# Attention with two mixing blocks on one core: fp32 scores for sixteen pairs, fp32 products for six, and shorter conversion and normalisation

## The chip, the cores and the metric

The kernel runs on one core of a Trainium2 chip. A core has a matrix engine (TensorE, PE in the rows; its weight loads are PEld), a vector engine (VectorE, DVE), a scalar engine (ScalarE, ACT), a general engine (GpSimd, POOL) and an engine that mostly issues transfers (SyncE, SP), and sixteen DMA engines behind the queues. Engines run their own instructions in order and wait for each other by semaphores. The metric is the time of one execution on the device in microseconds (us), as the median of several runs.

## The reference, cut to what matters

```python
def _attn_ref(q, k, v):                       # 4 batches, 12 heads, 448 tokens, 64 columns
    scores = np.matmul(q, k.transpose(0, 1, 3, 2)) / np.sqrt(64)
    scores = np.where(np.triu(np.ones((448, 448), bool), k=1), -1e9, scores)
    attn = np.exp(scores - np.max(scores, axis=-1, keepdims=True))
    attn = attn / (np.sum(attn, axis=-1, keepdims=True) + 1e-09)
    return np.matmul(attn, v)

def _moe_ref(x, w_tok1, w_tok2, w_ch1, w_ch2):   # x: 4 x 448 x 768
    xt = x.transpose(0, 2, 1)
    u = x + (np.maximum(xt @ w_tok1, 0.0) @ w_tok2).transpose(0, 2, 1)
    return u + np.maximum(u @ w_ch1, 0.0) @ w_ch2

def _moe2_ref(x, w_theta, w_tok_r, w_tok_i, w_ch):
    theta = x @ w_theta
    y = einsum('ts,bsd->btd', w_tok_r, x * cos(theta)) + einsum('ts,bsd->btd', w_tok_i, x * sin(theta))
    u = x + y
    return u + np.maximum(u @ w_ch, 0.0)
```

The three follow each other: attention, then token and channel mixing, then a second mixing block. q, k, v are float32; the weights of the mixing blocks arrive as 64-bit floats.

## The kernel before, in words

Two heads of a batch make a pair; there are 24 pairs, six to a batch. A pair has seven score tiles (`TILES`): tile (0, 0) holds the first 64 queries of both heads, and tiles (i, h), i = 1 to 3, hold 128 queries of one head against 64 + 128 i keys. One tile is one step, 168 steps in all. At step n the kernel emits `scores` of tile n and, `LAG` = 4 steps behind, `pv`, the product with v, of tile n - 4. Beside the steps it emits conversions of weights, and from step 53 on (`FIRST_UNIT`) units of the channel mixing: 14 up to step 88, then 29 in 42 steps. The scheduler of the language puts the instructions of each engine in order by priority; scores, `pv` and `prep` stand at a high priority (`AHEAD`).

`scores` multiplies q with k into a bank of PSUM; VectorE (L356) adds the mask and takes the row's extreme, ScalarE (L358) takes the exponential and its row sum. There are two forms of each matrix product:

- Scores: for pairs in `NATIVE` (0 to 7) q and k stay float32, 64 rows of contraction padded with zeros to 128 by a POOL memset (L275), one product a tile (L349). For the others `prep` loads q and k in 128 rows, ScalarE rounds both to fp32r, VectorE makes the rests (L291 to L296), and a tile has two products (L349, L351) of at least 256 columns.
- Products with v: for pairs in `NATPV` (0 to 11) TensorE transposes the exponentials in float32 (L365), ScalarE copies them out of PSUM (L367) and `pv` multiplies in float32 (L393). For the others ScalarE writes a high half in fp16 (`copy_to`, L160), VectorE the low halves (L378), SP issues a transposing DMA (L381), and `pv` makes three fp16 products a block (L403). These pairs need v in two halves as well: `value_squares` and `value_split`.

The products of a pair gather in one bank, `ps_pv`. `finish` divides them by the row sums `sm` into `xb`: the six tiles with i > 0 in one VectorE pass (L410), tile (0, 0) in two passes of 64 rows (L415), since its two heads stand in different rows. Every two pairs, `tokmix` uses `xb` and its two fp32r parts.

The weights arrive as 64-bit floats. ScalarE takes the high word, as a float, times a power of two (`abs64`); VectorE shifts the exponent into place (L183), adds the sign (L184) and the low word's upper bits (L185). Thirty weight tiles of 768 columns pass through it during attention (`ROUNDINGS`, one in some 3.4 steps from step 14, and six late ones), four of the token weights at the start, and 26 smaller pieces (384 or 224 columns) for the resident weights of the last block, near 525 to 575 us.

All bulk loads and stores, the transposing DMAs among them, are issued from SP's queue in one order.

Of the kernel before, what the change touches and what calls it, by code (L numbers as in the profile page):

```python
# [8 lines left out]
F32 = mybir.dt.float32  # L9
# [4 lines left out]
AF = mybir.ActivationFunctionType  # L14
# [15 lines left out]
NATIVE = {0, 1, 2, 3, 4, 5, 6, 7}  # L30
NATPV = {0, 1, 2, 3, 4, 5, 6, 7, 8, 9, 10, 11}
# [23 lines left out]
def fused(ctx, tc, q, k, v, w_tok1, w_tok2, w_ch1, w_ch2, w_theta, w_tok, w_ch, out):  # L55
# [119 lines left out]
    def abs64(f, raw):  # L175
        nc.scalar.activation(f, raw[:, :f.shape[-1], 1].bitcast(F32), AF.Abs, scale=REBIAS)

    def round64(f, raw):


        low, high = raw[:, :f.shape[-1], 0], raw[:, :f.shape[-1], 1]
        u = f.bitcast(U32)
        nc.vector.tensor_scalar(out=u, in0=u, scalar1=3, scalar2=None, op0=ALU.logical_shift_left)  # L183
        nc.vector.scalar_tensor_tensor(out=u, in0=high, scalar=0x80000000, in1=u, op0=ALU.bitwise_and, op1=ALU.bitwise_or)  # L184
        nc.vector.scalar_tensor_tensor(out=u, in0=low, scalar=29, in1=u, op0=ALU.logical_shift_right, op1=ALU.bitwise_or)  # L185
# [42 lines left out]
    def mm3(ps, a, b, ka, kb, first, last):  # L228
# [12 lines left out]
                            base=0, pattern=[[-1, P]], channel_multiplier=1)  # L241
    mask0 = ac.tile([P, 2, 64], F32, tag="mask0", name="mask0")
# [20 lines left out]
    for j in range(2):  # L263
        xb = ac.tile([P, 4, P], F32, tag=f"x{j}", name=f"x{j}")
        nc.gpsimd.memset(xb[:, 0, :], 0.0)
        xbufs.append(xb)
# [55 lines left out]
    class Pair:  # L322
        def __init__(self, b, pr, parts):
            self.b, self.pr = b, pr
            self.qs, self.kh, self.kl, self.v = parts[:4]
            self.unit = parts[4] if len(parts) > 4 else 1.0
            self.mx = ap2.tile([P, 7], F32, tag="mx", name="mx")
            self.sm = ap2.tile([P, 8], F32, tag="sm", name="sm")
            self.pts, self.ps, self.sent = {}, None, None
            self.native_pv = b * NPR + pr in NATPV  # L330

    def scores(pp, i, h):
# [17 lines left out]
        if pp.kl is not None:  # L350
# [8 lines left out]
                             accum_out=pp.sm[:, j:j + 1])  # L359
# [23 lines left out]

    def pv(pp, i, h):
        if pp.ps is None:
            pp.ps = bank("pv", 1)
        reg = 0 if i == 0 else ((i - 1) * 2 + h + 1) * D
        pt = pp.pts[i, h]
        if pp.native_pv:
            blks = [8] if i == 0 else [6 + h] + [2 * u + h for u in range(i)]  # L390
            n = D if i == 0 else 2 * D
            for u, vt in enumerate(blks):
                pp.pv = nc.tensor.matmul(pp.ps[:, reg:reg + n], lhsT=pt[:, u], rhs=pp.v[0][:, vt * D:vt * D + n],  # L393
                                 start=(u == 0), stop=(u == len(blks) - 1))
            return
# [6 lines left out]
        for n, (blk, c, vt) in enumerate(jobs):  # L402
            pp.pv = nc.tensor.matmul(pp.ps[:, reg:reg + D], lhsT=pt[:, blk], rhs=pp.v[c][:, vt * D:(vt + 1) * D],  # L403
                             start=(n == 0), stop=(n == len(jobs) - 1))

    def finish(pp, xb, xg):
        ps, sm = pp.ps, pp.sm
        nc.vector.tensor_scalar(out=sm[:, 0:7], in0=sm[:, 0:7], scalar1=1e-9, scalar2=pp.unit, op0=ALU.add, op1=ALU.mult)
        nc.vector.reciprocal(out=sm[:, 0:7], in_=sm[:, 0:7])
        nc.vector.tensor_tensor(out=xb[:, 1:4, :].rearrange("p i (h d) -> p (i h) d", h=2),  # L410
                                in0=ps[:, D:7 * D].rearrange("p (j d) -> p j d", d=D),
                                in1=sm[:, 0:6].unsqueeze(2).to_broadcast([P, 6, D]), op=ALU.mult)
        for h in range(2):
            r = slice(64 * h, 64 * h + 64)
            nc.vector.tensor_scalar(out=xb[r, 0, 64 * h:64 * h + 64], in0=ps[r, 0:D],  # L415
                                    scalar1=sm[r, 6:7], scalar2=None, op0=ALU.mult)
# [570 lines left out]
```

## Time and profile before

| what | value |
|---|---|
| median of 3 runs | 890.24 us (889.29 to 891.47) |
| the profiled execution | 888.24 us, of which its span is 886.5 us |
| granted TensorE clock, mean | 0.996 |
| busy in the span | TensorE 96%, VectorE 71%, ScalarE 61%, POOL 19% |

The span runs from the first instruction to the last of the profiled execution; busy is the time in which an engine has an instruction open. Matmuls overlap, and their ends are modelled, so an open TensorE is not a TensorE at its peak. L with a number is a line of the kernel before; a line can be that of a helper.

### The profile page before, as it was taken

Reading aid. Unit: us, or ns where it says so; the run is one execution under the profiler, and the core shown is the slowest. Engines: PE = TensorE matmul, PEld = TensorE weight load, DVE = VectorE, ACT = ScalarE, POOL = GpSimd, SP = SyncE. Lnnn points to the kernel's source line nnn. Section 1 sums busy time; section 2 is a strip of 40 time slices with the busy share of each in tenths; the row PEclk is TensorE's granted clock in tenths of the full one; section 3 lists DMA queues with packets and bytes.
Section 4 is the critical chain, followed back from the end, with each engine's and each line's share of the span. In section 5 each row is a group of like instructions: output and inputs, shape, how many; then the busy total and the mean of one; then the engine's idle time right before and its main releaser. Section 6 shows DMA issues by size and latency. Waiting matters only on the chain.

```text
span 886.5 us, 16065 instructions
## 1 busy us (share of the span) xinstructions
PE 851.7 (96%) x5619; PEld 547.8 (62%) x5619; DVE 632.8 (71%) x1511; ACT 544.0 (61%) x1271; POOL 166.3 (19%) x319
## 2 busy tenths in 40 slices
PE   7999889999899999999999999999999999999998
PEld 6888767776656566565666554555555555555554
DVE  6899996878998775766886258768856448567442
ACT  6798776757776564657655257437746447466441
POOL 2232232223251200121211112051111002101000
PEclk9999989999999999999999999999999999999999
DMA  7857865747899996656565778711622132231011
GB/s 217 255 182 228 289 231 183 272 169 232 205 310 306 288 210 148 165 202 129 162 186 137 232 240 293 238 55 41 201 62 67 50 116 67 69 116 58 18 50 73
DMA packets 105793, 149.63 MB, mean 169 GB/s; under 512 B 61104, under 2 KB 72304, under 8 KB 105712
## 3 DMA queue, kind: packets, MB, share of 16 engines
q1 hardware_dynamic: 105168, 147.59, 55.3%
q0 software_dynamic: 384, 0.79, 0.4%
q8 instruction: 44, 0.72, 0.3%
q14 instruction: 37, 0.30, 0.1%
q10 hardware_dynamic: 160, 0.23, 0.1%
HBM read 112.39 MB, written 22.81 MB: 153 GB/s over the span
## 4 chain that ended last, share of the span: by engine, by line
PE 66%; DVE 13%; DMA 11%; issue 4%; ACT 3%; POOL 1%; SPq 1%; ACTq 0%; DVEq 0%; POOLq 0%
PE ps_mm L230 15%; PE ps_mm L231 15%; PE ps_mm L232 15%; DMA pt<-ph 6%; PE ps_pv L393 3%; PE ps_sc L349 3%; PE ps_sc L230 3%; PE ps_sc L231 3%; PE ps_sc L232 3%; DVE sb L356 2%; DVE ph L378 1%; PE ps_mm L365 1%; DVE wf L184 1%; DMA ws<-w_c 1%; DVE wf L185 1%
## 5 line engine op out<-in xcount | busy, mean ns | idle before, releaser
L230 PE MATMUL ps_mm<-h,ws 128*128 128x448 f16 x432 | 151.9, 353 | 0.4 <-DMA ws<-w_c 0.4
L231 PE MATMUL ps_mm<-h,ws 128*128 128x448 f16 x432 | 152.2, 353 | 0.0
L232 PE MATMUL ps_mm<-h,ws 128*128 128x448 f16 x432 | 152.2, 353 | 0.0
L230 PEld LDWEIGHTS <-ws 128*128 128x128 f16 x720 | 70.4, 98 | 63.4 <-issue 4.1
L232 PEld LDWEIGHTS <-ws 128*128 128x128 f16 x720 | 70.4, 98 | 62.8 <-issue 3.1
L231 PEld LDWEIGHTS <-ws 128*128 128x128 f16 x720 | 70.5, 98 | 62.4 <-issue 4.2
L358 ACT ACTIVATE sb<-sb,mx 128x192 f32<-128x192 f32 (+3 forms) x168 | 89.2, 532 | 32.1 <-DVE mx L356 30.6
L230 PE MATMUL ps_mm<-ut,ws 128*128 128x448 f16 x288 | 102.0, 355 | 5.6 <-ACT ut L160 2.3
L231 PE MATMUL ps_mm<-ut,ws 128*128 128x448 f16 x288 | 102.0, 354 | 0.6 <-DVE ut L196 0.5
L232 PE MATMUL ps_mm<-ut,ws 128*128 128x448 f16 x288 | 102.1, 354 | 0.0
L356 DVE CUSTOM_DVE_ANT_0 sb<-ps_sc,mask 128x192 f32<-128x192 f32 (+3 forms) x168 | 74.3, 456 | 12.7 <-PE ps_mm L365 9.5
L124 ACT ACTIVATE junk<-acc 128x448 bf16<-128x448 f32 x72 | 41.1, 571 | 63.9 <-DVE acc L879 41.0
L160 ACT ACTIVATE ph<-sb 128x192 f16<-128x192 f32 (+3 forms) x84 | 36.4, 442 | 45.9 <-DMA pt<-ph 45.8
L393 PE MATMUL ps_pv<-v_raw,ptf 128*128 128x128 f32 (+1 forms) x456 | 63.9, 277 | 0.3 <-PE ps_mm L138 0.2
L378 DVE SCALAR_TENSOR_TENSOR ph<-sb,ph 128x64 f16<-128x64 f32 (+3 forms) x156 | 44.6, 328 | 26.4 <-ACT ph L160 26.2
L393 PEld LDWEIGHTS ps_pv<-v_raw,ptf 128*128 128x128 f32 x456 | 59.2, 193 | 5.0 <-PE ps_mm L138 1.5
L163 POOL TENSOR_SCALAR h<-t 128x448 f16<-128x448 f32 x48 | 32.8, 685 | 140.3 <-ACT t L477 140.1
L349 PE MATMUL ps_sc<-kh,qs 128*128 128x256 f32 (+2 forms) x112 | 45.9, 416 | 3.3 <-DVE mx L356 3.3
L230 PE MATMUL ps_sc<-th,ut 128*128 128x384 f16 x144 | 46.9, 326 | 0.0
L232 PE MATMUL ps_sc<-th,ut 128*128 128x384 f16 x144 | 46.8, 326 | 0.0
L231 PE MATMUL ps_sc<-th,ut 128*128 128x384 f16 x144 | 46.6, 326 | 0.0
L479 DVE TENSOR_TENSOR h<-t,h 128x448 f16<-128x448 f32 x48 | 30.2, 633 | 19.7 <-POOL h L163 19.5
(215 smaller groups left out, 2040.5 us busy)
## 6 DMA issues: line engine op xcount, KB each, us to landing
ws<-w_c SPq DMA_DIRECT2D x120, 384.0 KB, 4.5
raw<-in_w_ch_dram SPq DMA_DIRECT2D x30, 768.0 KB, 4.5
w_c<-ws SPq DMA_DIRECT2D x30, 384.0 KB, 3.5
q_raw<-in_q_dram SPq DMA_DIRECT2D x16, 448.0 KB, 4.1
k_raw<-in_k_dram SPq DMA_DIRECT2D x16, 448.0 KB, 4.9
v_raw<-in_v_dram SPq DMA_DIRECT2D x24, 288.0 KB, 3.2
x2d<-acc SPq DMA_DIRECT2D x24, 224.0 KB, 3.7
acc<-x2d SPq DMA_DIRECT2D x24, 224.0 KB, 2.8
```

The lines of the kernel that those rows point to most:

```text
L124: nc.scalar.activation(j[:, 0:src.shape[-1]], src, AF.Square, accum_out=dst)
L160: nc.scalar.activation(dst, src, AF.Copy, scale=scale)
L163: e.tensor_scalar(out=dst, in0=src, scalar1=scale, scalar2=0.0, op0=ALU.mult, op1=ALU.add)
L230: nc.tensor.matmul(ps, lhsT=ka(a[:, 0]), rhs=kb(b[:, 0]), start=first, stop=False)
L231: nc.tensor.matmul(ps, lhsT=ka(a[:, 0]), rhs=kb(b[:, 1]), start=False, stop=False)
L232: return nc.tensor.matmul(ps, lhsT=ka(a[:, 1]), rhs=kb(b[:, 0]), start=False, stop=last)
L349: nc.tensor.matmul(ps[:, 0:n], lhsT=lhs, rhs=cut(pp.kh), start=True, stop=pp.kl is None)
L356: pp.first = nc.vector.tensor_tensor_reduce(out=dst, in0=src, in1=msk, op0=ALU.add, op1=ALU.min, scale=-0.125, scalar=3.0e38, accum_out=pp ...
L358: pp.last = nc.scalar.activation(sb[:, 0:kk], sb[:, 0:kk], AF.Exp, bias=pp.mx[:, j:j + 1], scale=-1.0, accum_out=pp.sm[:, j:j + 1])
L378: nc.vector.scalar_tensor_tensor(out=dst, in0=sb[:, c0:c1], scalar=PSC, in1=hi[:, c0:c1], op0=ALU.mult, op1=ALU.subtract)
L393: pp.pv = nc.tensor.matmul(pp.ps[:, reg:reg + n], lhsT=pt[:, u], rhs=pp.v[0][:, vt * D:vt * D + n], start=(u == 0), stop=(u == len(blks) - 1))
L479: gates[0] = nc.vector.tensor_tensor(out=t[:, 1], in0=f, in1=t[:, 0], op=ALU.subtract)
```

## The change

Pairs 8 to 15 move to the float32 form of the scores, pairs 6 to 11 to the fp16 form of the product with v. `abs64` keeps the sign in the float that it makes and leaves on POOL a word that holds the sign alone, in place of the high word; `round64` then shifts and joins the sign in one pass. `finish` scales all of `ps_pv` in one pass: tile (0, 0)'s product is written twice, side by side, and a two-column mask `own`, multiplied on POOL with that tile's reciprocal sum, zeroes the half that belongs to the other head; `xb` needs no memset any more. In the float32 form the last tile's product is 64 columns wide instead of 128.

```diff
--- before.py
+++ after.py
@@ -27,8 +27,8 @@
 NEG = -1.0e30
 PSC = 32768.0
 BUFS = dict(ut=12, h2=8, acc=12, ws=8, wf=3, raw=3, sb=3, ph=3, pt=5, t=3, junk=1)
-NATIVE = {0, 1, 2, 3, 4, 5, 6, 7}
-NATPV = {0, 1, 2, 3, 4, 5, 6, 7, 8, 9, 10, 11}
+NATIVE = {0, 1, 2, 3, 4, 5, 6, 7, 8, 9, 10, 11, 12, 13, 14, 15}
+NATPV = {0, 1, 2, 3, 4, 5}
 AHEAD, LAG, LOOK = 500, 4, 2
 KEEP, UBACK = 6, 16
 ROUND_BITS, ROUND_FETCH, ROUND_SPLIT, ROUND_STORE = 1, 2, 3, 5
@@ -173,15 +173,16 @@
         nc.sync.dma_start(out=raw[:, :src.shape[-1]].rearrange("p n w -> p (n w)"), in_=src.bitcast(U32))
 
     def abs64(f, raw):
-        nc.scalar.activation(f, raw[:, :f.shape[-1], 1].bitcast(F32), AF.Abs, scale=REBIAS)
+        high = raw[:, :f.shape[-1], 1].bitcast(F32)
+        nc.scalar.activation(f, high, AF.Copy, scale=REBIAS)
+        product(high, high, 0.0, 1.0)
 
     def round64(f, raw):
 
 
-        low, high = raw[:, :f.shape[-1], 0], raw[:, :f.shape[-1], 1]
+        low, sign = raw[:, :f.shape[-1], 0], raw[:, :f.shape[-1], 1]
         u = f.bitcast(U32)
-        nc.vector.tensor_scalar(out=u, in0=u, scalar1=3, scalar2=None, op0=ALU.logical_shift_left)
-        nc.vector.scalar_tensor_tensor(out=u, in0=high, scalar=0x80000000, in1=u, op0=ALU.bitwise_and, op1=ALU.bitwise_or)
+        nc.vector.scalar_tensor_tensor(out=u, in0=u, scalar=3, in1=sign, op0=ALU.logical_shift_left, op1=ALU.bitwise_or)
         nc.vector.scalar_tensor_tensor(out=u, in0=low, scalar=29, in1=u, op0=ALU.logical_shift_right, op1=ALU.bitwise_or)
 
     def wf_tile():
@@ -239,6 +240,10 @@
     nc.gpsimd.memset(mask, 0.0)
     nc.gpsimd.affine_select(out=mask[:, 320:448], in_=mask[:, 320:448], compare_op=ALU.is_ge, fill=NEG,
                             base=0, pattern=[[-1, P]], channel_multiplier=1)
+    own = ac.tile([P, 2], F32, tag="own", name="own")
+    nc.vector.memset(own, 0.0)
+    for h in range(2):
+        nc.vector.memset(own[64 * h:64 * h + 64, h:h + 1], 1.0)
     mask0 = ac.tile([P, 2, 64], F32, tag="mask0", name="mask0")
     nc.vector.tensor_copy(mask0.rearrange("p a b -> p (a b)"), mask[:, 320:448])
     nc.vector.memset(mask0[64:128, 0, :], NEG)
@@ -262,7 +267,6 @@
     xbufs = []
     for j in range(2):
         xb = ac.tile([P, 4, P], F32, tag=f"x{j}", name=f"x{j}")
-        nc.gpsimd.memset(xb[:, 0, :], 0.0)
         xbufs.append(xb)
 
     loads = {}
@@ -325,7 +329,7 @@
             self.qs, self.kh, self.kl, self.v = parts[:4]
             self.unit = parts[4] if len(parts) > 4 else 1.0
             self.mx = ap2.tile([P, 7], F32, tag="mx", name="mx")
-            self.sm = ap2.tile([P, 8], F32, tag="sm", name="sm")
+            self.sm = ap2.tile([P, 10], F32, tag="sm", name="sm")
             self.pts, self.ps, self.sent = {}, None, None
             self.native_pv = b * NPR + pr in NATPV
 
@@ -356,7 +360,7 @@
         pp.first = nc.vector.tensor_tensor_reduce(out=dst, in0=src, in1=msk, op0=ALU.add, op1=ALU.min, scale=-0.125,
                                        scalar=3.0e38, accum_out=pp.mx[:, j:j + 1])
         pp.last = nc.scalar.activation(sb[:, 0:kk], sb[:, 0:kk], AF.Exp, bias=pp.mx[:, j:j + 1], scale=-1.0,
-                             accum_out=pp.sm[:, j:j + 1])
+                             accum_out=pp.sm[:, 2 + j:3 + j])
         if pp.native_pv:
             nt = 1 + i
             c0 = 64 if i == 0 else 0
@@ -381,16 +385,20 @@
         pp.sent = nc.sync.dma_start_transpose(out=pt[:, 0:nb, :], in_=ph[:, 0:nb * P])
         pp.pts[i, h] = pt
 
+    def twice(ap):
+        return ap.unsqueeze(1).to_broadcast([P, 2, D])
+
     def pv(pp, i, h):
         if pp.ps is None:
             pp.ps = bank("pv", 1)
-        reg = 0 if i == 0 else ((i - 1) * 2 + h + 1) * D
+        reg = 0 if i == 0 else ((i - 1) * 2 + h + 2) * D
         pt = pp.pts[i, h]
         if pp.native_pv:
             blks = [8] if i == 0 else [6 + h] + [2 * u + h for u in range(i)]
-            n = D if i == 0 else 2 * D
             for u, vt in enumerate(blks):
-                pp.pv = nc.tensor.matmul(pp.ps[:, reg:reg + n], lhsT=pt[:, u], rhs=pp.v[0][:, vt * D:vt * D + n],
+                n = 2 * D if reg < 7 * D else D
+                rhs = twice(pp.v[0][:, vt * D:(vt + 1) * D]) if i == 0 else pp.v[0][:, vt * D:vt * D + n]
+                pp.pv = nc.tensor.matmul(pp.ps[:, reg:reg + n], lhsT=pt[:, u], rhs=rhs,
                                  start=(u == 0), stop=(u == len(blks) - 1))
             return
         if i == 0:
@@ -400,20 +408,17 @@
             for u in range(i):
                 jobs += [(1 + u, 0, 2 * u + h), (1 + u, 1, 2 * u + h), (1 + i + u, 0, 2 * u + h)]
         for n, (blk, c, vt) in enumerate(jobs):
-            pp.pv = nc.tensor.matmul(pp.ps[:, reg:reg + D], lhsT=pt[:, blk], rhs=pp.v[c][:, vt * D:(vt + 1) * D],
+            rhs = pp.v[c][:, vt * D:(vt + 1) * D]
+            pp.pv = nc.tensor.matmul(pp.ps[:, reg:reg + (2 * D if i == 0 else D)], lhsT=pt[:, blk], rhs=twice(rhs) if i == 0 else rhs,
                              start=(n == 0), stop=(n == len(jobs) - 1))
 
     def finish(pp, xb, xg):
         ps, sm = pp.ps, pp.sm
-        nc.vector.tensor_scalar(out=sm[:, 0:7], in0=sm[:, 0:7], scalar1=1e-9, scalar2=pp.unit, op0=ALU.add, op1=ALU.mult)
-        nc.vector.reciprocal(out=sm[:, 0:7], in_=sm[:, 0:7])
-        nc.vector.tensor_tensor(out=xb[:, 1:4, :].rearrange("p i (h d) -> p (i h) d", h=2),
-                                in0=ps[:, D:7 * D].rearrange("p (j d) -> p j d", d=D),
-                                in1=sm[:, 0:6].unsqueeze(2).to_broadcast([P, 6, D]), op=ALU.mult)
-        for h in range(2):
-            r = slice(64 * h, 64 * h + 64)
-            nc.vector.tensor_scalar(out=xb[r, 0, 64 * h:64 * h + 64], in0=ps[r, 0:D],
-                                    scalar1=sm[r, 6:7], scalar2=None, op0=ALU.mult)
+        nc.vector.tensor_scalar(out=sm[:, 2:9], in0=sm[:, 2:9], scalar1=1e-9, scalar2=pp.unit, op0=ALU.add, op1=ALU.mult)
+        nc.vector.reciprocal(out=sm[:, 2:9], in_=sm[:, 2:9])
+        product(sm[:, 0:2], own, sm[:, 8:9], 1.0)
+        nc.vector.tensor_tensor(out=xb.rearrange("p i (h d) -> p (i h) d", h=2), in0=ps.rearrange("p (j d) -> p j d", d=D),
+                                in1=sm[:, 0:8].unsqueeze(2).to_broadcast([P, 8, D]), op=ALU.mult)
         pr2 = pp.pr % 2
         c = slice(pr2 * P, (pr2 + 1) * P)
         copy_to(pick("xhi"), xg[0][:, :, c], xb)
```

## Rows read from the trace of the kernel before

**Rows 1.** The page's first part: busy time, share of the span, instructions.
```profile
PE 851.7 (96%) x5619; PEld 547.8 (62%) x5619; DVE 632.8 (71%) x1511; ACT 544.0 (61%) x1271; POOL 166.3 (19%) x319
```

**Rows 2.** Stretches: PE, PEld, DVE, ACT, POOL busy (records), granted clock, DMA share, GB/s.
```profile
0.00:80.00 80.00, 73.35 (x499) 63.20 (x500) 67.78 (x192) 62.22 (x172) 24.21 (x47) 1.00 0.72 220
80.00:138.00 58.00, 52.47 (x346) 41.46 (x346) 52.76 (x121) 46.11 (x113) 18.41 (x31) 0.94 0.76 259
138.00:206.00 68.00, 67.99 (x469) 52.35 (x468) 53.60 (x126) 45.20 (x113) 13.74 (x26) 1.00 0.60 212
206.00:292.00 86.00, 79.94 (x607) 53.43 (x606) 79.13 (x210) 61.00 (x155) 27.88 (x44) 1.00 0.93 264
292.00:515.00 223.00, 215.35 (x1630) 136.27 (x1628) 148.65 (x414) 125.14 (x315) 33.88 (x70) 1.00 0.69 182
515.00:575.00 60.00, 56.59 (x313) 30.45 (x313) 44.22 (x108) 36.36 (x83) 8.82 (x16) 1.00 0.80 264
```

**Rows 3.** Timeline of TensorE, a pair with fp32 products: start, length, records.
```profile
61.72 1.06 PE L393 MATMUL ps_pv<-v_raw,ptf 128*128 128x128 f32 x8
...
66.62 0.28 PE L429 MATMUL ps_mm<-xg,wt 128*128 128x256 f32 x1
66.74 0.28 PE L430 MATMUL ps_mm<-xg,wt 128*128 128x256 f32 x1
...
71.60 0.60 PE L365 MATMUL ps_mm<-ident,sb 128*128 128x128 f32 x4
```

**Rows 4.** Timeline of TensorE at its longest wait after the start.
```profile
116.16 0.53 PE L230 MATMUL ps_mm<-ut,ws 128*128 128x448 f16 x1 [2.32 <-ACT ut L160]
```

**Rows 5.** A stretch right behind it, columns as in rows 2.
```profile
116.00:123.00 7.00, 6.34 (x26) 4.84 (x26) 6.62 (x16) 6.36 (x15) 1.13 (x4) 0.51 0.96 344
```

**Rows 6.** Timeline of TensorE, the products of one tile from halves.
```profile
402.37 0.19 PE L403 MATMUL ps_pv<-v_hi,pt 128*128 128x64 f16 x1
...
402.99 0.19 PE L403 MATMUL ps_pv<-v_hi,pt 128*128 128x64 f16 x1
```

**Rows 7.** ScalarE's groups by line.
```profile
L160 ACT ACTIVATE ph<-sb 128x192 f16<-128x192 f32 (+3 forms) x84 | 36.4, 442 | 45.9 <-DMA pt<-ph 45.8
...
L367 ACT ACTIVATE ptf<-ps_mm 128x256 f32<-128x256 f32 (+3 forms) x84 | 36.0, 449 | 11.8 <-PE ps_mm L365 11.4
...
L160 ACT ACTIVATE qs<-q_raw 128x896 fp32r<-128x896 f32 x16 | 15.0, 938 | 0.4 <-DMA q_raw<-in_q_dram 0.4
```

**Rows 8.** VectorE's groups by line: records, busy, mean ns, idle before.
```profile
L378 DVE SCALAR_TENSOR_TENSOR ph<-sb,ph 128x64 f16<-128x64 f32 (+3 forms) x156 | 44.6, 328 | 26.4 <-ACT ph L160 26.2
...
L317 DVE SCALAR_TENSOR_TENSOR v_raw<-v_raw,sv,v_hi 128x576 f16<-128x576 f32 x12 | 11.1, 922 | 1.0 <-POOL v_hi L163 1.0
...
L167 DVE TENSOR_TENSOR qs<-q_raw,qs 64x896 fp32r<-64x896 f32 x16 | 17.9, 1117 | 0.5
...
L167 DVE TENSOR_TENSOR kl<-k_raw,kh 128x896 fp32r<-128x896 f32 x16 | 17.4, 1088 | 6.6 <-ACT kh L160 6.4
...
L183 DVE TENSOR_SCALAR wf<-wf 128x768 uint32<-128x768 uint32 x30 | 20.1, 670 | 1.2 <-ACT wf L176 1.2
...
L410 DVE TENSOR_TENSOR x<-ps_pv,sm 128x384 f32<-128x384 f32 x24 | 13.3, 552 | 1.3 <-PE ps_mm L439 0.7 <-PE ps_pv L403 0.4
...
L415 DVE TENSOR_SCALAR x<-ps_pv,sm 64x64 f32<-64x64 f32 x48 | 13.4, 279 | 0.4
```

**Rows 9.** The tile ph: idle time until, who waited, microseconds to landing.
```profile
  DMA pt<-ph: 45.8, 38
...
  PE ps_pv L403: 6.1, 10
...
DMA to landing us min/median/max: 2.3/3.5/9.0
```

**Rows 10.** Single lines: ns min/median/max of a POOL and a VectorE pass.
```profile
L163 POOL TENSOR_SCALAR ws<-wf,s x24: 908/911/2427, 37.5 to 261.3; 128x768 f16<-128x768 f32 x24
...
L184 DVE SCALAR_TENSOR_TENSOR wf<-raw,wf x34: 623/956/1549, 12.1 to 458.2; 128x768 uint32<-128x768 uint32 x30, 128x512 uint32<-128x512 uint32 x2, 128x448 uint32<-128x448 uint32 x2
```

## The prediction

> **What bounds the kernel now.** I read the page's busy times first: TensorE has a record open in 96% of the span, VectorE in 71% [rows 1]. That makes TensorE the bound on average, so I cut the span into stretches, to see where it is not [rows 2]. I cut where pairs of heads begin (VectorE's first pass over their scores): pair 6 at 80 us, 9 at 138, 12 at 206, 16 at 292; the last ends before 515. In the first stretch (pairs 0 to 5) TensorE is open for 73.4 of 80 us. From 80 to 138 us it is open for 52.5 of 58 with VectorE at 52.8; from 138 to 206 it is full, VectorE at 53.6 of 68; from 206 to 292 VectorE has 79.1 of 86 (92%), the DMA engines 0.93. Behind 292 TensorE is nearly full to the end.
>
> An open record is not work, though. A record of 128 fp32 columns is 0.278 us long, but eight of them together take 1.06, so they follow each other at (1.06 - 0.28) / 7 = 0.112 us; an fp32 product leaves two such records, a transpose one (four in 0.60, again 0.11 us). An fp32r record of 256 columns starts 0.12 us after the one before it [rows 3]. So short waits hide behind the tails of records, and the work is better counted in spacings: 0.87 ns a column in each of the two fp32 records, 1.75 a product, and 0.46 for fp32r. The reader should see two things: TensorE's work sets the time wherever channel units fill it, and in 0 to 138 and 206 to 292 us the chain from scores over VectorE and ScalarE sets it.
>
> One place shows what a wait does: TensorE stands 2.3 us until ScalarE's first ut [rows 4], and in the seven us from there the granted clock is 0.51, the lower of the two levels, 1.2 GHz [rows 5].
>
> **The change, part by part.** *Scores of pairs 8 to 15 in fp32.* Split, a pair streams 2 x (256 + 2 x 256 + 2 x 320 + 2 x 448) = 4608 fp32r columns, 2.1 us; in fp32 128 + 2 x (192 + 320 + 448) = 2048 columns at 1.75 ns, 3.6 us. Eight pairs add about 12 us to TensorE. ScalarE loses two copies of 0.94 us a pair [rows 7], 15 us; VectorE two rests of 1.12 and 1.09 [rows 8], 2.2 a pair, 17.7 us. POOL gains two memsets a pair, a pair ahead of use, and SP reads half the bytes for q and k.
>
> *Products of pairs 6 to 11 from fp16 halves.* Before, a pair has 19 transposes (19 x 0.11 = 2.1 us) and 19 fp32 products (38 records, 4.1 us together). From halves it has 51 records; 22 starts of one tile lie between 402.37 and 402.99, 0.03 us each [rows 6], so 1.5 us. TensorE is relieved of 4.6 us a pair, 28 us in all. ScalarE trades 7 copies of 0.449 for 7 of 0.442 [rows 7] and gains one pass of squares a pair (576 columns, under the 0.94 of 896). VectorE gains 13 low halves (156 x 0.328 / 12 = 4.3 us a pair) and the rest of v, 0.92 [rows 8]; with 0.4, an estimate, for the one-column passes of its scale 5.6; six pairs, 34 us. SP gains seven transposing DMAs a pair. They land after 3.5 us (2.3 to 9.0); ScalarE has stood 45.8 us for a free ph and TensorE 6.1 us for a pt, over twelve such pairs [rows 9]. So expect some 3 us of such waits on TensorE from six more; waits on ph cost nothing while ScalarE has room.
>
> *Conversion.* Each of the thirty weights of 768 columns loses VectorE's shift, 0.67 us [rows 8]; twelve fall into pairs 0 to 5, twelve into 6 to 11 (one in 3.4 steps), 8 us each. The two passes that stay keep their price: the fused one has the same inputs and size. POOL gains a pass over the high words, which I price at its nearest row, the scaled copy of 768 elements, 0.91 us [rows 10]. It stands a step ahead of VectorE's use, and POOL is 19% busy [rows 1]; so nothing on the path. Bounds: nothing, and the row's longest, 2.4 us, late at each conversion, hidden by the step.
>
> *One normalisation.* The 384-column pass and two of 64 (0.55 + 2 x 0.28 = 1.11) become one of 512; scaled by columns 0.69 us. VectorE saves 0.4 us a pair. A product on POOL comes between reciprocal and pass; if nothing of VectorE's other work stands between, that hop eats the gain, bounds -0.4 and +0.5 us a pair. Tile (0,0) writes 128 columns instead of 64: 0.1 us a pair. In fp32 pairs the last tile falls from 128 to 64 columns in four products, 0.45 us less.
>
> **Sum.** TensorE: +12 - 28 - 6 x 0.33 + 18 x 0.08 = -17 us. How much arrives is asked stretch by stretch.
>
> Pairs 0 to 5: TensorE -2; VectorE falls from 67.8 to 57.3 (-8 -2.5), and I take 2 us of hidden waits with it: -4 (0 to -7).
>
> Pairs 6 to 11, 126 us: TensorE would need 22 us less, but VectorE, at 106.4, becomes 106.4 + 34 - 8 - 11 (five pairs' rests) - 2.5 = 119. At the 92% that it reached from 206 to 292, that is 129 us, 3 more than now. Conversions yield to scores and may slip by up to a pair; two of them (2.9 us each with the passes that stay and the ws rest) go into the next stretch, which leaves 113 / 0.92 = 122. So -4, between -13 (VectorE filled, 113 us) and +8 (nothing slips, and 88%, as DMA and VectorE queue for each other).
>
> Pairs 12 to 15: TensorE +6, VectorE 79 to 68 (three pairs' rests, shifts, normalisation), DMA lighter; half of the waits (6 us open to see) go: +2.5 (-1 to +6).
>
> Pairs 16 to 23: TensorE +0.6, VectorE -3.4: -0.5 (-3 to +1). From 515 to 575 VectorE loses 26 shorter shifts where TensorE stands open 56.6 of 60 us: -0.5 (-2 to +2). Behind it: nothing changes.
>
> Together -6.5 us. The profiled execution took 888.24 us (span 886.5), 2.0 under the median of 890.24, so 881.7 there and 883.7 against the median; I say 883.5. From no change a measurement tells about 0.3%, 2.7 us.
>
> **The rivals.** *All of TensorE's relief arrives* (-17 and more: 872). For it: the 92% need not be VectorE's ceiling, and conversions can slip. Against it: 119 us of VectorE's work in 126.
>
> *No difference* (within 2.7 us). Pairs 6 to 11 are VectorE's, their -4 is 0, and pairs 12 to 15 pay the full +6.
>
> *Slower through the clock.* In pairs 6 to 8 TensorE's work falls by some 12 of 52 us, with no channel units until step 53, and its waits for pt come where steps are 2 us long. The one comparable wait, 2.3 us, brought 7 us at 1.2 GHz [rows 4, 5], worth 3.5 us. It decides from three such stretches on: -6.5 + 3 x 3.5 + 3 us of pt waits in the same place gives +7, 897. Against it: pairs 12 to 17 waited for pt and kept 1.00 [rows 2]. The Trainium skill (TensorE: Matmul & The Clock Gate, "HAM oscillation — how this bites in real kernels") says that a matmul stream broken by DMA waits falls back to the lower clock again and again; the low stretch here agrees, the clock of 1.00 from 206 to 292 us beside pt waits does not.
>
> *Slower through POOL.* If each new pass kept VectorE off for its 0.91 us, a conversion would cost +0.24 rather than -0.67: VectorE's 113 in pairs 6 to 11 becomes 124 and, at 0.92, 135 us, +9 instead of -4; pairs 0 to 5 lose their -2, total +9, 899. Against it: POOL's copies run beside VectorE now, yet half of its two-input passes stay within 0.956 us and the longest is 1.55 [rows 10]. The Trainium skill (SBUF — State Buffer, "Who interferes with whom") has it that a VectorE instruction with two SBUF inputs and a POOL one that reads SBUF block each other for whole instructions; the spread of both rows agrees that some are held, not most.
>
> **How the numbers follow.** Forecast 0.58, all of the relief 0.08, no difference 0.16, clock 0.12, POOL 0.06. Faster 0.66, same 0.16, slower 0.18. The range takes the first three with the bounds of the terms and half of the slower ones: 868 to 894.
>
> **What would show it.** The ends of pairs 5, 11 and 15 against 80, 206 and 292 us; L349 on k_pad with 224 records; VectorE's busy time near 610 us (632.8 + 34 - 18 - 10, and some 30 for all shifts), TensorE's waits for pt no more than 10 us, and the granted clock between 80 and 140 us. It is wrong if pairs 6 to 11 take over 130 us, or if a new wait on POOL (own, or the high words) shows on VectorE.

## The result, and the profile after

The changed kernel takes 896.76 us (median of four runs, 895.28 to 897.44), the kernel before 889.88 beside it: ratio 1.0069 [1.0041, 1.0097], slower by 0.7%. I had said 883.5 us, 868 to 894, and slower with 0.18. The sign is wrong and the time lies outside the range. The profiled execution took 897.41 us (span 895.6) at a mean granted clock of 0.982; before it was 888.24 at 0.996.

The page's first part, answering to [rows 1]:

```profile
PE 848.2 (95%) x5595; PEld 528.2 (59%) x5595; DVE 616.6 (69%) x1486; ACT 534.7 (60%) x1267; POOL 244.3 (27%) x435
```

VectorE was to come to some 610 us and came to 616.6; TensorE still has a record open 95% of the time. Nothing on this line tells of a loss. The stretches do; cut again where pairs 6, 9, 12 and 16 begin (81.1, 141.7, 195.0 and 298.0 us now), columns as in [rows 2]:

```profile
0.00:81.00 81.00, 73.60 (x510) 63.71 (x511) 62.14 (x177) 63.08 (x177) 39.92 (x64) 1.00 0.72 222
81.00:141.70 60.70, 50.52 (x356) 34.82 (x354) 54.37 (x148) 45.25 (x118) 33.29 (x53) 0.86 0.88 244
141.70:195.00 53.30, 47.51 (x349) 30.49 (x348) 45.37 (x132) 33.25 (x91) 24.13 (x37) 0.97 1.00 254
195.00:298.00 103.00, 93.66 (x683) 58.58 (x682) 82.61 (x220) 64.91 (x168) 46.14 (x72) 1.00 0.89 247
298.00:526.00 228.00, 220.11 (x1625) 139.10 (x1623) 144.17 (x387) 124.15 (x311) 38.47 (x81) 0.98 0.70 180
```

Pairs 0 to 5 take 1.0 us more (forecast -4), though VectorE has 62 us of work there instead of 68. Pairs 6 to 11 end 12.4 us sooner (126.3 to 113.9; forecast -4), but pairs 12 to 15 take 103.0 instead of 85.8 (+17.2; forecast +2.5): channel units and VectorE's work slipped across the cut. Pairs 6 to 15 together went from 212.1 to 216.9 us, +4.8 where I had -1.5. From pair 16 on it is +3.3 where I had -1.0. The three sum to +9.1, the change of the span.

The clock stands out. Of six stretches at the lower level, 1.2 GHz, the first three lie here, one in the second row and two in the third (the first row is what came before):

```profile
85.00:89.00 4.00, 2.02 (x12) 1.37 (x11) 4.00 (x12) 3.29 (x10) 2.72 (x5) 1.00 0.08 27
89.00:96.00 7.00, 6.78 (x31) 5.48 (x32) 6.62 (x19) 4.78 (x13) 4.44 (x6) 0.51 0.55 141
...
106.00:120.00 14.00, 9.86 (x49) 4.89 (x48) 13.44 (x30) 12.56 (x30) 10.41 (x16) 0.63 1.08 285
```

In the four microseconds ahead of the first, TensorE is open for 2.0 and VectorE for all 4.0. All low stretches last 30.7 us, against 6.8 before. The stream of products is what I had counted, TensorE's groups by line:

```profile
L353 PE MATMUL ps_sc<-k_pad,q_raw 128*128 128x192 f32 (+3 forms) x224 | 80.0, 454 | 14.1 <-DVE mx L360 6.5 <-DMA q_raw<-in_q_dram 6.0 <-POOL h L163 1.6
...
L412 PE MATMUL ps_pv<-v_hi,pt 128*128 128x64 f16 (+1 forms) x576 | 41.2, 195 | 8.1 <-DMA pt<-ph 5.3 <-DVE x L420 2.7
L412 PE MATMUL ps_pv<-v_raw,pt 128*128 128x64 f16 (+1 forms) x342 | 35.1, 195 | 0.0
```

224 fp32 score records were forecast. 918 records of fp16 products are 18 pairs of 51; 228 records of fp32 products (L401) and 114 of transposes (L369) are six pairs of 38 and 19.

To say where a span goes I use one account from here on. **Work** is TensorE's records, each counted by the spacing of its kind (fp32 and fp32r as in the prediction, fp16 0.03 us for 64 columns, 0.19 for 448). **Clock** is the length of each low stretch times one minus its granted clock. **Rest** is what remains of the span: TensorE waits, for whatever reason, and any error of the spacings. Before: 814.8 + 3.4 + 68.2. After: 799.6 + 15.8 + 80.2. TensorE was relieved of 15.2 us (forecast 17), and that was paid back in clock (+12.4) and rest (+12.0). Work hangs on how the spacings are rounded: with the rounded ones printed here it comes to 827.6 before and 810.5 after, 17.1 less instead of 15.2. So two or three microseconds of work or rest tell nothing.

### The profile page after: what moved, and what is told of

Its sections match the earlier page's. It is cut to its first block, busy times and chain, and to the rows that moved or that the text cites. A ratio compares the mean times of both kernels' runs of the same rounds, so it can differ in the third digit from the quotient of the medians.

```text
span 895.6 us, 16298 instructions
## 1 busy us (share of the span) xinstructions
PE 848.2 (95%) x5595; PEld 528.2 (59%) x5595; DVE 616.6 (69%) x1486; ACT 534.7 (60%) x1267; POOL 244.3 (27%) x435
## 4 chain that ended last, share of the span: by engine, by line
PE 64%; DMA 17%; ACT 7%; DVE 6%; issue 4%; POOL 2%; SPq 1%; ACTq 0%; POOLq 0%; DVEq 0%
PE ps_mm L231 15%; PE ps_mm L232 14%; PE ps_mm L233 14%; DMA pt<-ph 11%; PE ps_sc L353 4%; PE ps_sc L231 3%; PE ps_sc L232 3%; PE ps_sc L233 3%; DMA ws<-w_c 2%; ACT junk L124 2%; DVE ph L382 2%; PE ps_pv L401 2%; ACT ph L160 1%; ACT sb L362 1%; PE ps_pv L412 1%
## 5 line engine op out<-in xcount | busy, mean ns | idle before, releaser
L362 ACT ACTIVATE sb<-sb,mx 128x320 f32<-128x320 f32 (+3 forms) x168 | 89.4, 534 | 29.2 <-DVE mx L360 28.6
L382 DVE SCALAR_TENSOR_TENSOR ph<-sb,ph 128x64 f16<-128x64 f32 (+3 forms) x234 | 69.7, 340 | 39.3 <-ACT ph L160 39.0
L353 PE MATMUL ps_sc<-k_pad,q_raw 128*128 128x192 f32 (+3 forms) x224 | 80.0, 454 | 14.1 <-DVE mx L360 6.5
L160 ACT ACTIVATE ph<-sb 128x192 f16<-128x192 f32 (+3 forms) x126 | 54.1, 442 | 60.0 <-DMA pt<-ph 59.5
L360 DVE CUSTOM_DVE_ANT_0 sb<-ps_sc,mask 128x320 f32<-128x320 f32 (+3 forms) x168 | 74.5, 455 | 11.8 <-PE ps_mm L369 6.0
L759 POOL TENSOR_SCALAR tmp<-tmp 128x384 f32<-128x384 f32 x28 | 15.5, 554 | 147.5 <-ACT tmp L758 144.5
L353 PEld LDWEIGHTS ps_sc<-k_pad,q_raw 128*128 128x128 f32 x224 | 38.4, 202 | 25.8 <-DVE mx L360 12.0
L412 PEld LDWEIGHTS <-pt 128*128 128x128 f16 x918 | 36.2, 98 | 22.9 <-DMA pt<-ph 10.9
L412 PE MATMUL ps_pv<-v_hi,pt 128*128 128x64 f16 (+1 forms) x576 | 41.2, 195 | 8.1 <-DMA pt<-ph 5.3
L231 PE MATMUL ps_sc<-th,ut 128*128 128x384 f16 x144 | 46.9, 326 | 0.0
L233 PE MATMUL ps_sc<-th,ut 128*128 128x384 f16 x144 | 46.8, 326 | 0.0
```

The source lines that it names most:

```text
L160: nc.scalar.activation(dst, src, AF.Copy, scale=scale)
L231: nc.tensor.matmul(ps, lhsT=ka(a[:, 0]), rhs=kb(b[:, 0]), start=first, stop=False)
L233: return nc.tensor.matmul(ps, lhsT=ka(a[:, 1]), rhs=kb(b[:, 0]), start=False, stop=last)
L353: nc.tensor.matmul(ps[:, 0:n], lhsT=lhs, rhs=cut(pp.kh), start=True, stop=pp.kl is None)
L360: pp.first = nc.vector.tensor_tensor_reduce(out=dst, in0=src, in1=msk, op0=ALU.add, op1=ALU.min, scale=-0.125, scalar=3.0e38, accum_out=pp ...
L362: pp.last = nc.scalar.activation(sb[:, 0:kk], sb[:, 0:kk], AF.Exp, bias=pp.mx[:, j:j + 1], scale=-1.0, accum_out=pp.sm[:, 2 + j:3 + j])
```

## The experiments

All ratios are against the kernel before, run beside each (its medians there were 889.9 to 891.5 us), and kernels are compared by them. The table gives the account of each profiled execution, in us; where none is given here, the text says what was read.

| kernel | median us | ratio [95%] | span | work | clock | rest |
|---|---|---|---|---|---|---|
| before | 889.88 | 1 | 886.5 | 814.8 | 3.4 | 68.2 |
| after | 896.76 | 1.0069 [1.0041, 1.0097] | 895.6 | 799.6 | 15.8 | 80.2 |
| p1_products | 901.6 | 1.0129 [1.0109, 1.0149] | 898.1 | 788.2 | 24.8 | 85.0 |
| p2_scores | 889.3 | 0.9982 [0.9967, 0.9998] | 887.8 | 826.7 | 3.4 | 57.7 |
| u1_products12 | 887.34 | 0.9963 [0.9939, 0.9987] | 885.3 | 823.8 | 0.9 | 60.5 |
| u2_products8 | 888.51 | 0.9965 [0.9940, 0.9991] | 886.1 | 807.7 | 6.2 | 72.3 |
| w1_fill_6_8 | 898.67 | 1.0080 [1.0054, 1.0105] | 896.2 | 806.6 | 17.0 | 72.5 |
| z1_fill_6_7 | 897.99 | 1.0067 [1.0043, 1.0092] | 895.9 | 812.3 | 8.5 | 75.0 |
| x3_low_on_pool | 894.45 | 1.0042 [1.0016, 1.0068] | 886.1 | 799.6 | 8.5 | 77.9 |
| x1_ph4 | 885.42 | 0.9937 [0.9919, 0.9955] | 884.5 | 799.6 | 13.6 | 71.2 |
| y1_before_ph4 | 880.67 | 0.9885 [0.9865, 0.9906] | 880.1 | 814.8 | 5.1 | 60.6 |
| y2_pv8_ph4 | 879.77 | 0.9874 [0.9854, 0.9894] | 877.6 | 807.7 | 4.0 | 65.8 |

**The four parts, each alone on the kernel before.**

```diff
 p1_products:  -NATPV = {0, ..., 11}
               +NATPV = {0, 1, 2, 3, 4, 5}
 p2_scores:    -NATIVE = {0, ..., 7}
               +NATIVE = {0, ..., 15}
 p3_convert:   the new abs64 and round64 alone
 p4_finish:    the new finish, twice, own and the narrower last tile alone
```

> The kernel before with the fp16 products of pairs 6 to 11 alone. Clock theory (pairs 6 to 8 leave TensorE too thin, the granted clock falls to 1.2 GHz, and most of the relief is lost): the page's granted clock shows low stretches between 85 and 125 us, some 15 to 20 us of them where before has 7, and the time is 886 to 896 us. Scores theory (the loss comes from the fp32 scores of pairs 8 to 15): faster than before by 6 us or more, 884 or less. POOL theory (the conversion's pass on POOL is the loss): also faster, 884 or less.

> The kernel before with the fp32 scores of pairs 8 to 15 alone. Clock theory: TensorE works 12 us more and VectorE 18 less, half of the 12 is given back by shorter waits: 890 to 897. Scores theory: the 12 us and more arrive, 899 to 904. POOL theory: as the clock theory, for the memsets are ahead of their use.

> The kernel before with the lighter conversion alone (sign word on POOL, one VectorE pass less). Clock theory: a gain of 2 to 5 us, 885 to 888, with VectorE some 30 us less busy. POOL theory: VectorE waits for the POOL pass or is held off by it, 892 to 898. Scores theory: as the clock theory.

> The kernel before with the single normalisation pass, the doubled tile (0,0) and the narrower last tile alone. Clock theory: -0.45 us on TensorE in twelve pairs and +0.1 in all, VectorE -10 us: 885 to 889. POOL theory: the product with own puts POOL between VectorE's two passes; if its queue is behind, the bank of products is free later and the time is 891 to 894. Scores theory: as the clock theory.

p1_products is slower by 1.3%, p2_scores gains 0.2% (889.3 us; the scores theory had 899 to 904), p3_convert gains 0.5% (885.06 us, 0.9946 [0.9931, 0.9961]; the POOL theory had 892 to 898), p4_finish makes no difference (889.43 us, 0.9994 [0.9976, 1.0012]). The four ratios multiply to 1.0050, within the interval of the whole change: the parts add up, and the loss is that of the products. For p1 the clock theory had the low stretches right (17 us between 85 and 125 us) and the time too low: 901.6 us for 886 to 896. Of p1, the stretch of pairs 6 to 8, which took 58.5 us before:

```profile
79.40:148.40 69.00, 49.25 (x343) 34.51 (x343) 65.94 (x170) 51.26 (x126) 25.29 (x38) 0.80 0.91 243
```

VectorE is busy for 65.9 of 69 us, the clock is 0.80, and TensorE, relieved of 26.6 us in all, is open for 49. p2 shows the reverse: 11.9 us more TensorE work, 10.5 less rest, and no time lost.

**The products of fewer pairs, on the changed kernel.**

```diff
 u1_products12:  -NATPV = {0, 1, 2, 3, 4, 5}
                 +NATPV = {0, ..., 11}
 u2_products8:   +NATPV = {0, ..., 7}
```

> The changed kernel with the fp32 products of pairs 6 to 11 put back (NATPV 0 to 11), all else of the change kept. If the parts add up as they did alone (0.998 x 0.995 x 0.999), 0.992: 881 to 886. Clock theory: the low stretches between 85 and 125 us are gone, at most 7 us of 1.2 GHz in all. Wait theory (the fp16 products cost by VectorE and the transposing DMAs, whatever the clock): the same time, but TensorE's waits for pt before 200 us gone, and low stretches may stay.

> The changed kernel with fp32 products for pairs 0 to 7, so that TensorE stays filled until the channel units begin in pair 7. Clock theory: no low stretch before 120 us, the relief of pairs 8 to 11 (18 us of TensorE) arrives in part: 876 to 886, at or under the kernel with twelve. Wait theory: half-way between the changed kernel and the one with twelve, 886 to 892.

Both are faster than before, and alike; u1 missed the 881 to 886 us that the parts promised, and u2 the clock theory's 876 to 886. So pairs 8 to 11 may have fp16 products at no cost, though without gain either, and what costs 1.0% (1.0069 against 0.9965) is to give them to pairs 6 and 7 as well. Whether two other pairs, as the last of six, would cost the same was not tried. Of u2, pairs 6 to 8, 9 to 11, 12 to 15 and 16 to 23:

```profile
80.30:128.60 48.30, 44.11 (x311) 34.97 (x311) 42.28 (x108) 39.22 (x105) 27.29 (x42) 1.00 0.69 219
128.60:191.10 62.50, 53.67 (x397) 36.43 (x396) 51.03 (x143) 38.90 (x104) 30.96 (x43) 0.95 0.99 252
191.10:294.70 103.60, 97.68 (x697) 60.84 (x696) 83.38 (x216) 64.17 (x165) 43.20 (x72) 0.98 0.87 246
294.70:510.00 215.30, 207.84 (x1575) 131.25 (x1574) 142.09 (x386) 121.52 (x305) 39.60 (x81) 1.00 0.71 185
```

Pairs 6 to 8 fall from 60.6 us to 48.3, with VectorE's busy time from 54.3 to 42.3 and the clock at 1.00. Much of that slips into pairs 9 to 11; by pair 16 the gain is 3.3 us, and the other 6.9 come up to 510 us, where the changed kernel lost 5.1 us to two low stretches and u2 none; so the gain at the end was not all earned in these pairs. Work is 8.1 us more than after and the span 9.5 less.

**Useless TensorE work as a filler.** If the lower clock, and not the waiting, is what costs, work that keeps TensorE going should bring time back; if another chain sets the pace, it should be free.

```diff
+        if pp.b * NPR + pp.pr in (6, 7, 8):      # w2: (12, 13, 14); z1: (6, 7)
+            for _ in range(3):                   # z1: 8
+                w = 512 - reg
+                nc.tensor.matmul(pp.ps[:, reg:512], lhsT=ones, rhs=ones[:, 0:64].unsqueeze(1).to_broadcast([P, w // 64, 64]), start=True, stop=True)
```

> The changed kernel with useless bf16 products added ahead of each tile's product with v in pairs 6 to 8 (three times the free rest of the bank, 5568 columns or 2.3 us a pair, 7 us in all; their results are overwritten, so nothing of the computation changes). Clock theory: the low stretches from 85 to 125 us shrink from 17 us to 7 or less, which gives back 5 us or more, and the added work partly fills waits: 888 to 896, not slower in spite of 7 us more work. Wait theory: TensorE's time there is not what counts, so 896 to 899; if the work is not hidden, up to 904.

> Control: the same 7 us of useless products in pairs 12 to 14, where the granted clock is 1.00 in the changed kernel and channel units fill TensorE. Clock theory: nothing to give back, 899 to 904. Wait theory: as in pairs 6 to 8, so the two fills give the same time.

> The changed kernel with useless bf16 products ahead of each tile's product with v in pairs 6 and 7, eight times the free rest of the bank (14848 columns, 6.2 us a pair, 12 us in all, more than the 9 us that the fp16 products took off TensorE there; results overwritten, nothing of the computation changes). Clock theory (pairs 6 and 7 cost 8 us because TensorE, too thin there, drops to 1.2 GHz): less than 7 us of low clock before 125 us, and 888 to 895 in spite of the added work. If the waits of pairs 6 and 7 cost by themselves, whatever the clock: the clock may come back, the time stays at 896 or more.

w1 and w2 (897.3 us, 1.0059 [1.0032, 1.0086]) add 7 us of work and, beside the changed kernel's 1.0069, 0.1% and -0.1% of time: there is room for it in either place, as the wait theory had it (w1 at 896 to 899 us; the clock theory had w2 at 899 to 904). In w1 the clock did not recover (low for 13.6 us up to 125 us, for 17.0 in the changed kernel), so w1 decides nothing on the clock. z1 adds 12.7 us in pairs 6 and 7 alone, and there it did. Pairs 6 to 8:

```profile
80.00:138.60 58.60, 51.48 (x400) 34.96 (x400) 50.00 (x142) 41.20 (x109) 29.33 (x46) 0.94 0.93 222
```

The clock of pairs 6 to 8 rises from 0.86 to 0.94 (low for 6.8 us before 125 us, where the changed kernel has 17.0), the time lost to it over the span falls from 15.8 to 8.5 us, and the ratio is that of the changed kernel (1.0067 for 1.0069): what the expectation had set for waits that cost by themselves. In the account 12.7 us of work went in, 7.3 of clock and 5.2 of rest went out, and the span stayed. With the clock as the cause and the filler hidden it would have been 7 us less; with both on the path 5 more. A filler half on the path beside a clock that costs is not excluded, though 7 us were free in w1 and w2. Locally time did come back: pairs 6 and 7 take 34.0 us for 39.1. But VectorE did 26.9 us of work there for 36.1; the rest moved on, and by pair 16 z1 is 6.1 us behind the changed kernel (304.1 for 298.0). Part of VectorE's work gives way, so the length of one stretch does not tell what a change is worth at the end.

**The links of the chain.** A tile with fp16 products goes score, extreme (VectorE), exponential and high half (ScalarE), low halves (VectorE), transposing DMA, product. In pairs 6 to 8 of the changed kernel this takes 11.5 us a tile on average, from VectorE's first pass over the scores to the landing: extreme and exponential 2.3, wait and high half 1.8, low halves 2.6, issue 0.7, the transfer 4.05. Who waited for whom from 81 to 142 us (us in total, times, longest):

```profile
PEld L412 <- DMA pt<-ph: 3.8, 5, 1.2
...
ACT ph L160 <- DMA pt<-ph: 1.8, 4, 0.5
```

So the waits for a free ph, 59.5 us over the span, hardly fall into these pairs; what is full there is VectorE, 54.4 of 60.7 us. I took the links one by one on the changed kernel.

```diff
 x1_ph4:         -BUFS = dict(..., ph=3, pt=5, ...)
                 +BUFS = dict(..., ph=4, pt=5, ...)
 x2_lag6:        -AHEAD, LAG, LOOK = 500, 4, 2      and pt=5
                 +AHEAD, LAG, LOOK = 500, 6, 2      and pt=7, one buffer for kl
 x3_low_on_pool, pairs 6 to 11:
                 -nc.vector.scalar_tensor_tensor(out=dst, ...)
                 +nc.gpsimd.memset(dst, 0.0)
 x4_short_dma, pairs 6 to 11:
                 +nb = 1 + i
                 +jobs = [j for j in jobs if j[0] < 1 + i]
```

> The changed kernel with four ph buffers instead of three. Latency theory (a tile with fp16 products needs 10 to 16 us from its score to its product, only four tiles are under way at a time, so pairs 6 to 8 step at a quarter of that): ScalarE's waits for a free ph (59.5 us in all) fall, but the chain of a tile shortens little: 892 to 897. ScalarE theory (the waits on ph hold the exponentials up): 886 to 891.

> The changed kernel with the product with v six steps behind the scores instead of four, seven pt buffers for it, and for their room one buffer of kl instead of two (kl is first used in pair 16). Latency theory: the same chain spread over six steps: pairs 6 to 8 start to start (60.6 us in the changed kernel) fall to 52 us or less, low stretches before 125 us to 7 us or less, 884 to 891. VectorE theory (VectorE's work in pairs 6 to 8 fills the time): pairs 6 to 8 stay within 2 us of 60.6, 894 to 899.

> The changed kernel without the low halves of pairs 6 to 11: POOL writes zeros in their place, so that part of the computation is left out; products and DMAs stay. VectorE loses 4.3 us a pair, 26 in all, and the tile's chain some 3 us of its 12. VectorE theory: pairs 6 to 8 fall by 10 us or more, 882 to 888. Latency theory: by a quarter of the time they spend without channel units, 8 to 12 us as well, 884 to 890. If the DMA or POOL sets the pace: 893 or more.

> The changed kernel with the transposing DMAs of pairs 6 to 11 cut to the first 1 + i blocks (19 of 32 blocks a pair) and the products that need the others left out, so that part of the computation is left out; VectorE still computes all low halves. DMA theory (the sixteen DMA engines, 0.88 to 1.00 busy from 81 to 195 us, set the pace): 884 to 890. Latency theory: a landing of 4.5 us falls to some 3.5, one twelfth of the chain: 891 to 896. VectorE theory: 895 to 897.

x2 gives 892.36 us (1.0040 [1.0013, 1.0066]), x4 893.19 (1.0022 [1.0003, 1.0040]): 0.3 and 0.5% under the changed kernel, neither back at the kernel before. The latency theory had x2 at 884 to 891 us with pairs 6 to 8 in 52 (they take 55.1), so it missed; the DMA theory missed x4 (884 to 890). x2 is 16.9 us ahead where pair 16 begins, at 281.1 us, and 5.6 at the end of the span; by the account's spacings TensorE had done some 15 us less of its work by then, and kl, used from there on, has one buffer, so it is no clean test. x3 is 0.3% under it, over runs from 887.9 (granted clock 0.990) to 899.0 (0.982). The profiled one is that of 887.9; its pairs 6 to 8:

```profile
80.30:128.00 47.70, 38.83 (x278) 27.09 (x278) 38.83 (x102) 37.53 (x101) 32.60 (x76) 0.93 0.94 246
```

With VectorE's work down by 15.5 us the stretch is 12.9 us shorter, as a VectorE limit would have it, but pairs 9 to 11 then take 64.6 us for 53.3, and of 18 us taken from VectorE over pairs 6 to 15 the profiled execution keeps 4.6 by pair 16, and the median over the whole 0.3%, some 2.5 us, where both the VectorE and the latency theory had 882 to 890. So VectorE's low halves are one link, not the whole cause. x1 alone gains much, 1.3%, with 52.6 us of ScalarE's waits for a ph instead of 59.5; 885.4 us is under the latency theory's 892 to 897 and next to the 886 to 891 of ScalarE's waits for a ph. A theory that the third ph buffer is what the change ran out of would then have the fourth do nothing for the kernel before.

```diff
 y1: before, ph=4     y3: p1_products, ph=4
 y2: u2_products8, ph=4     y4: u1_products12, ph=4
 z2: z1_fill_6_7, ph=4
```

> The kernel before with four ph buffers. Buffer theory (a tile of the fp16 products waits for one of three ph, and the change put six more such pairs where weight conversions already load VectorE, ScalarE and the DMA engines): before has this only behind pair 12, where channel units cover it, so 887 to 891. If a fourth ph is worth the same 11 us to any kernel of this family: 876 to 882.

> The changed kernel with fp32 products for pairs 0 to 7 and four ph buffers (888.5 with three). Buffer and clock theory together: pairs 6 and 7 keep the clock and pairs 8 to 11 keep their relief, 878 to 884, the fastest so far. If neither is what holds pairs 8 to 11: 885 to 889, as its neighbours.

> The fp16 products of pairs 6 to 11 alone, with four ph buffers (901.6 with three). Buffer theory: 887 to 893, most of the part's 12 us gone. Clock theory (the part's loss is the lower clock in pairs 6 to 8): the low stretches stay and so does the time, 897 or more.

> The changed kernel with fp32 products for pairs 0 to 11 and four ph buffers (887.3 with three). Buffer theory: little is left to win without the six pairs, 883 to 888; the fp16 products then are no gain and no loss beside 885.4 of the changed kernel with four. If a fourth ph helps any kernel: 875 to 880.

> The same filling in the changed kernel with four ph buffers (885.4 without the filling; 879.8 with fp32 products in pairs 6 and 7). Clock theory: 879 to 884. Waits by themselves: 885 or more.

That theory falls: y1 gains 1.15% as well. ScalarE's waits for a ph in y1, where [rows 9] have 45.8:

```profile
  DMA pt<-ph: 27.3, 24
```

The profiled execution of y1 gains 6.4 us of span, and all of it lies in pairs 16 to 23 (216.6 to 209.4 us from pair 16's start to the last product with v), whose scores and products have the same form in the kernels before and after. With four buffers the order of the kernels stays: y2 879.77 and y4 880.21 (0.9884 [0.9864, 0.9904]) beside x1's 885.42, so pairs 6 and 7 still cost 0.6%, and again pairs 8 to 11 neither cost nor gain; the products alone, y3 (894.33 us, 1.0040 [1.0022, 1.0058]) over y1, cost 1.6%, between the 887 to 893 us of the buffer theory and the clock theory's 897 or more. z2 (895.04 us, 1.0050 [1.0030, 1.0070]) is 1.1% over x1, far from the clock theory's 879 to 884: its pairs 6 and 7 lose nothing to the clock, where x1's lose 6.5 us, and they are 3.9 us shorter, but with the fourth buffer most of the filler's 12.7 us is paid by the end. y2 and y4 are the best versions; y2 beats the kernel before by 1.3% and the changed one by 1.9%.

## Why the prediction was wrong

**The streams were right.** Products -26.6 us of TensorE work in p1 (forecast -28), scores +11.9 in p2 (forecast +12), -15.2 in all (forecast -17), within the error of the account. TensorE's waits for a pt are 5.3 us, where six more pairs were to add 3 to [rows 9]; ScalarE's waits for a ph rose to 59.5:

```profile
  DMA pt<-ph: 59.5, 50
...
  PE ps_pv L412: 5.3, 12
```

**Conversion had the right size, and the POOL rival was wrong.** The new POOL pass (L130) was priced at 0.91 us and takes that; VectorE's pass has the same median as in [rows 10]. But one sign of being wrong did appear: VectorE waits 9.4 us for the new pass, at 12 of 34 tiles, so it does not stand a step ahead of its use. From the tile of the raw weights, the time of single instructions (ns, least, median, most) and who waited for the new pass; then two single instructions at 107.9 us (start, length):

```profile
L130 POOL TENSOR_SCALAR raw<-raw x34: 607/907/1589, 12.0 to 467.3; 128x768 f32<-128x768 f32 x30, 128x512 f32<-128x512 f32 x2, 128x448 f32<-128x448 f32 x2
L185 DVE SCALAR_TENSOR_TENSOR wf<-wf,raw x34: 622/952/1654, 12.7 to 469.0; 128x768 uint32<-128x768 uint32 x30, 128x512 uint32<-128x512 uint32 x2, 128x448 uint32<-128x448 uint32 x2
...
  DVE wf L185: 9.4, 12
...
107.88 0.92 POOL L163 TENSOR_SCALAR ws<-wf,s 128x768 f16<-128x768 f32 x1
...
107.95 1.65 DVE L185 SCALAR_TENSOR_TENSOR wf<-wf,raw 128x768 uint32<-128x768 uint32 x1 [0.53 <-POOL raw L130]
```

Alone, the part gains 0.5%. The Trainium skill (SBUF — State Buffer, "Who interferes with whom") would have such passes hold each other off for whole instructions. The trace agrees: in the last two lines VectorE's pass begins 0.07 us after a POOL pass began and ends 0.80 us after that one ended, 1.65 us long where the median is 0.95. All eight long ones (1.16 to 1.65 us) of VectorE's sixty two-input passes on 768 columns end some 0.80 us after a POOL pass under which they began. They cost 3.6 us in all, where eleven cost 4.3 before, and only one of the eight began under the new pass. So the rival was wrong because the new pass seldom meets VectorE's, not because they do not hold each other off.

**The normalisation's price was right, its gain was not kept.** One pass takes 0.685 us (I had 0.69), and the part alone moves nothing, where I had taken 2.5 us off VectorE in each of two stretches as if part of it arrived.

```profile
L420 DVE TENSOR_TENSOR x<-ps_pv,sm 128x512 f32<-128x512 f32 x24 | 16.4, 685 | 1.1 <-PE ps_mm L444 0.5 <-PE ps_pv L412 0.4
```

**The step that failed** is "two of them go into the next stretch, which leaves 113 / 0.92 = 122. So -4", with its companion "+2.5" for pairs 12 to 15. I sized pairs 6 to 15 by VectorE's sum over the share it had reached once. The sum held (182 us; 119 + 68 = 187 forecast), the share did not: 84% of 216.9 us, for the 89% that my terms came to. (The division itself gives 123, so -3.) The rows by stretch show two things. In pairs 6 to 8 VectorE did reach 90%, but in pairs 9 to 15 only 82% (128.0 of 156.3 us), with TensorE open for 90%. And far more than two conversions slipped: pairs 6 to 11 hold 99.7 us of VectorE's work where I had 113, pairs 12 to 15 82.6 where I had 68, and TensorE's work there is some 13 us more than before, where I had 6. That is why pairs 6 to 11 beat my -4 and pairs 12 to 15 lost it again.

The sum says nothing of order: in pairs 6 and 7, with hardly a channel unit yet to fill TensorE (their first product starts at 112.5 us), each tile must pass VectorE twice, ScalarE twice and a transfer of 4 us. The fp32 path that it replaced has, behind the exponential, only TensorE and one ScalarE copy. So TensorE's relief was worth nothing where it was given: u2, with 8.1 us of it taken back, is 1.0% faster, and 7 to 12.7 us of useless work could be put in its place within 0.1%. That giving these two pairs fp16 products, beside pairs 8 to 11, is what costs is shown with three buffers (the changed kernel, u1, u2) and with four (x1, y2, y4). Why it costs stays open. That the waiting chain as a whole, and no single link, sets it is one reading that fits x2, x3 and x4, which give back 0.3, 0.3 and 0.5 of the 1.0%; it is not shown link by link, the ranges set for it were missed by x1, x2 and x3, and z1 shows that part of what fills VectorE there is work that can wait.

**Pairs 0 to 5** failed in the same manner on a smaller scale: "2 us of hidden waits" were to go with VectorE's shifts. VectorE's work fell by 6 us and the stretch rose by 1; rest there is some 13 to 18 us in every kernel of this study. So VectorE's busy time is not what sets that stretch.

**From pair 16 on** the forecast had no clock; two low stretches (at 368.9 and 440.6 us) lost 5.1 us, which is more than the difference between +3.3 and -1.0.

**The clock rival** gave 897 and had the place right: six low stretches, three of them in pairs 6 to 8, where TensorE is underused. That its figure met the median is in part luck: the 3 us of waits for a pt that it counted did not come (5.3 us for 6.1). The Trainium skill (TensorE: Matmul & The Clock Gate, "HAM oscillation — how this bites in real kernels") says that a stream broken by DMA waits falls back again and again; the 30.7 us of low stretches agree, but the waits of pairs 6 to 8 are for VectorE (L360, L420) as much as for transfers. And z1 took half of the loss away and no time of the whole with it, so the clock as the whole cause is not borne out. Its share stays open. Over thirteen kernels with three buffers (z1 left out) the median goes up by 0.70 us for each us lost to the clock (the median over a kernel's executions). Executions of one kernel, whose work is the same, differ alike: u2's go from 885.6 us at 0.996 to 893.3 at 0.987, and over 156 executions of eighteen kernels it is 0.63 us for each us lost. Both could be the mark of waiting as well as its cause. A few us between two of these kernels may also come from the order of instructions, which the scheduler makes anew for each; no run separates that.

## What to carry to other kernels

Relief of the engine that is busiest on average is worth its price only in a stretch where that engine's queue is full; ask, pair by pair, what else TensorE would have to do while a longer path over VectorE, ScalarE and a transfer runs. A sum of busy time over a share reached elsewhere is no forecast for a stretch whose work can move into the next one; follow both engines, stretch by stretch, to the end. Where a part of a change is a set of places, try it at a boundary further on: without two pairs of six all of the loss was gone.

## What was unexpected of the hardware

- One more ph buffer, where transposing transfers take 3.5 us to land, brings the kernel before to a ratio of 0.9885 [0.9865, 0.9906], a larger gain than that of any part of the change; why in pairs 16 to 23 was not pursued.
- 7 us of useless products on TensorE cost 0.1% in one place and -0.1% in another, which is nothing that the intervals can tell.
- The profiled clock was 0.972 to 0.985 in the kernels with fp16 products in pairs 6 and 7, but for x3 and the 12.7 us fillers (0.988 to 0.990 there), and 0.993 to 0.999 in all others.
